# Experts' last tiles cut to 64 tokens, token lists gathered ahead, and the run-time loop moved behind the experts' last product

## The chip, the cores and the metric

The program runs on one core of a Trainium2 chip. The metric is device time in microseconds (us) of one execution; lower is better. The core has a matrix engine (PE, or TensorE), a vector engine (DVE), an activation engine (ACT), a general engine (POOL, which issues the gathers and scatters) and a sync engine (SP, which issues the other transfers), each with its own queue of instructions, and 16 DMA engines.

## The reference

Three layers in a row; what the kernel must compute is this, in float32:

```python
# block attention: 8 batches x 8 heads, 576 positions in chunks of 64, 64 wide
attn = softmax(q_c @ k_c.T / 8);  out = attn @ v_c          # inside a chunk
x = out as [4608 tokens, 512]
# mixture of experts: every token goes to one of 8 experts
logits = x @ w_gate;  expert_idx = argmax(logits);  gate_w = softmax(logits)[expert_idx]
ye = relu(x[mask] @ w1[e]) @ w2[e]                          # 512 -> 1024 -> 512
x = gate_w * ye
# MLP: 512 -> 2048 -> 512, piecewise quadratic activation
h = x @ w_in
g = where(h >= 1, h, where(h <= -1, 0, (h + 1) ** 2 / 4))
out = g @ w_out
```

## The kernel before, in words

Every float32 operand of the expert and MLP products is scaled by a power of two and written as a sum of two fp16 numbers, `high` (L109, on ACT) and `low` (L112, on DVE: the rest after the high part). A product is made of three: high by high, high by low and low by high. Tokens go in tiles of 128.

**Attention** takes 36 steps of 128 tokens. In a step PE makes scores (L456), transposes (`t`, L464; `tx`, L484), the weighted values (`ob`, L476) and the gate's logits (`la`), DVE the maxima and normalised rows (L500 to L520), ACT the exponential `p` (L504). Steps are gathered to seven batches of the gate; after each, DVE works out every token's expert and its place in that expert's list, and POOL scatters the token numbers into the lists (L617).

**Experts** are taken by rank, the sizes being known only at run time. The token tiles are cut into 13 windows (rank r, first tile k, number of tiles): (0,0,3), (0,3,3), (1,0,4), (2,0,3), (2,3,3), (3,0,4), (4,0,3), (4,3,3), (5,0,4), (6,0,3), (6,3,2), (7,0,3), (7,3,2); they are called w0 to w12 here. `CAPS` holds each rank's tiles. `fetch(w)` gathers the list (L163) and the tokens' rows (`xg`, L140), takes the row maxima (`xam`, L100), scales and splits them (`xh`, L109 and L112), and the transposed tiles `xtw` come by DMA (L159). `ffn` then makes a window's first layer, 8 groups of 12 matmuls (L932), each left by ACT (`ht` high, L937) and DVE (`ht` low, L938), and its second layer, 24 matmuls of 512 columns to a tile (L966). `leave` copies a tile out of PSUM (ACT, L954), takes its maximum (`ym`, DVE) and scatters it (POOL, L958); in most windows this is done in the window behind.

Beside the windows a planner runs generators (`background`) that fetch and split the experts' weights, fetch the next window, and load the MLP's weights (`load_mlp`). Instructions are placed in the queues in the order in which the planner lets them go, by modelled clocks of the engines (`clk`), prices (`yield`, `spend`) and constants: `LIST` and `ROWS` are the modelled landing times of a list and of the rows. `load_mlp` ends in 16 conversions: `high` of a row of `mlpw`, then `low`, and then only the next row's `high`, since it writes over the row that the `low` before reads.

Tokens above an expert's cap go through `overflow()`, a loop whose trip count is read at run time (L992, L994). Every engine meets at a barrier there. With the reference's inputs the experts hold, by rank, 649, 506, 688, 452, 657, 417, 621 and 618 tokens, so that the loop makes no trip. Before the loop all of `background` is drained into the queues: `before_last` does so and calls `overflow`. The loop stands between the two layers of w12. The MLP (L1117, L1145) follows, in ten groups.

Of the kernel before, what the change touches and what calls it, by code (L numbers as in the profile page):

```python
# [29 lines left out]
CAPS = (6, 4, 6, 4, 6, 4, 5, 5)  # L30
BATCH = (6, 6, 6, 4, 6, 5, 3)
# [9 lines left out]
LIST, ROWS, WEIGHTS = 2.2, 3.0, 4.5  # L41
SLACK = 0.3, 0.6
# [12 lines left out]
def build(ctx, tc, qT, kT, v1, wg, w1, w2, wi, wo, out):  # L55
# [12 lines left out]
    with tc.manual_schedule(engines={E_.PE, E_.Activation, E_.DVE, E_.SP}):  # L68
# [114 lines left out]

        def fetch(w):

            r, k, size = windows[w]
            if k == 0 or w == 1:
                yield 0.1, 0.0
                spend(0.0, 0.0, 1.05)
# [9 lines left out]
            at = [clk["pool"] + ROWS - 1.05 * (size - 1 - t) for t in range(size)]  # L199
# [154 lines left out]
        with ExitStack() as ph:  # L354
# [70 lines left out]
            for r in range(E):  # L425
                pool.memset(capt[:, r:r + 1], float(CAPS[r] * P))
# [60 lines left out]
            def vector_work(i):  # L487
# [39 lines left out]
                if 0 <= i - 4 < NT:  # L527
# [3 lines left out]
                    spend(0.0, 0.65)  # L531
                slot(1.15)
                yield

            la = ps_l.tile([P, 512], F32, name="la")
            acc = la[:, 128:128 + (GB + 1) * E].rearrange("p (t e) -> p t e", e=E)
# [9 lines left out]
            def by_token(i):  # L546

                b, t = WHERE[i]
                if t == 0:
                    LG[b] = la[:, b % 2 * 64:b % 2 * 64 + GB * E].rearrange("p (t e) -> p t e", e=E)  # L550
                pe.matmul(LG[b][:, t, :], lhsT=LT.pop(i), rhs=sel4, start=True, stop=True)

            def gate(b):
                n = BATCH[b]
                lg = LG.pop(b)[:, 0:n]
# [188 lines left out]
        def gate_tail():  # L744
# [18 lines left out]
            ready[0] = 2  # L763
            for _ in range(20):
                yield
            overflow_plan()
# [3 lines left out]
        def overflow_plan():  # L770
# [5 lines left out]
            dve.tensor_tensor(out=nr, in0=nr, in1=capt, op=ALU.subtract)  # L776
# [3 lines left out]
            dve.tensor_scalar(out=nw, in0=nr, scalar1=float(P - 1), scalar2=0.0, op0=ALU.add, op1=ALU.max)  # L780
# [66 lines left out]
        with ExitStack() as ph:  # L847
# [71 lines left out]
            def ffn(r, xt, nt, ids, gates, i_x, beside=None, after=None, last=False, between=None, c0=0):  # L919

                N = nt * P
# [23 lines left out]
                if between:  # L945
                    between()
# [3 lines left out]
                ys = [ps_y.tile([P, 512], F32, name=f"y{t}", tag=f"y{t}") for t in range(min(nt, 3))] + more_ys[:max(0, nt - 3)]  # L950

                def leave(t):
                    y = yp.tile([P, D], F32, name="y", tag="y")
                    act.activation(out=y, in_=ys[t], func=AF.Copy, scale=gt[:, t:t + 1])  # L954
                    ym = small.tile([P, 1], F32, name="ym", tag="ym")
                    absmax(ym, y)
                    dve.tensor_tensor(out=ymax, in0=ymax, in1=ym, op=ALU.max)
                    ins = pool.indirect_dma_start(out=yd, out_offset=bass.IndirectOffsetOnAxis(ap=ids[t], axis=0), in_=y, in_offset=None,  # L958
# [17 lines left out]
                if not last:  # L976
# [10 lines left out]
            def overflow():  # L987
# [6 lines left out]
                with tc.For_i(0, n_over, 1):  # L994
# [9 lines left out]
                    dve.scalar_tensor_tensor(out=tmp, in0=capt, scalar=1.0 / P, in1=csum[:, 0:E], op0=ALU.mult, op1=ALU.subtract)  # L1004
# [29 lines left out]
                    ffn("over", xt, 1, [ix[:, 0:1]], ix[:, 1:2].bitcast(F32), i_x, last=True, c0=c_over)  # L1034
# [167 lines left out]
```

## Time and profile before

| | |
|---|---|
| three runs | 1375.74, 1376.52 and 1385.33 us; median 1376.52 |
| the profiled execution | 1387.27 us, its span 1385.3 us |
| PE busy | 1325.9 us, 96% of the span |
| DVE, ACT, POOL busy | 55%, 43%, 11% |
| granted PE clock, mean | 0.985 of full speed |
| stages | attention to about 190 us, experts to 634, MLP to the end |

The span is what the trace covers; the execution's own time is 2 us longer. The profiled execution lies 10.75 us above the median of the three runs, and one of the three is as long. The trace shows which engine an idle engine waited for; as PE is busy nearly throughout, its few idle stretches are the first thing to look for, and the rate of its products the second.

### The profile page before, as it was taken

What the parts mean: (1) busy time and instruction counts of PE and PEld (TensorE: products, weight loads), DVE (VectorE), ACT (ScalarE), POOL (GpSimd) and SP (SyncE); (2) the same over time, 40 slices, a digit from 0 to 9 for tenths busy, and PEclk for the clock granted to TensorE, in tenths of its full rate; (3) what the DMA queues carried; (4) which work ended last, traced back from release to release, by engine and by line L of the source; (5) the groups of instructions that cost most, each with busy time, mean ns of one, the idle gap of its engine ahead of it and who ended that gap; (6) DMA issues with size and microseconds to landing.
All of it is one profiled execution on the core that took longest, in us unless ns stands there. A gap on an engine that the chain in (4) does not pass through costs nothing.

```text
span 1385.3 us, 20006 instructions
## 1 busy us (share of the span) xinstructions
PE 1325.9 (96%) x7735; PEld 697.8 (50%) x7735; DVE 766.2 (55%) x1545; ACT 593.9 (43%) x1000; POOL 151.9 (11%) x190
## 2 busy tenths in 40 slices
PE   7888788999999999989999999999999999999998
PEld 5666653445445445555444444444444444444555
DVE  5558655678678777756464270724518064370723
ACT  3446433666666766644242240413315042240522
POOL 3111231221231222310000000000000000000000
PEclk9999899999999999999999999999999999999999
DMA  9989636666667663312111111111110111111000
GB/s 242 286 265 279 161 91 197 206 206 232 192 204 239 174 207 109 98 52 77 31 53 31 62 22 35 35 31 61 31 61 1 31 61 31 54 23 37 22 26 16
DMA packets 123201, 147.99 MB, mean 107 GB/s; under 512 B 89164, under 2 KB 89164, under 8 KB 121056
## 3 DMA queue, kind: packets, MB, share of 16 engines
q1 hardware_dynamic: 115264, 127.40, 32.6%
q0 software_dynamic: 7840, 19.29, 4.1%
q8 instruction: 62, 1.02, 0.3%
q14 instruction: 35, 0.29, 0.1%
HBM read 99.10 MB, written 29.72 MB: 93 GB/s over the span
## 4 chain that ended last, share of the span: by engine, by line
PE 55%; ACT 0%; issue 0%
PE h L1117 27%; PE o L1145 27%; PE y L966 1%; ACT y L954 0%; ACT ot L1138 0%
## 5 line engine op out<-in xcount | busy, mean ns | idle before, releaser
L1117 PE MATMUL h<-xtw,mlpw 128*128 128x512 f16 (+2 forms) x1920 | 375.1, 358 | 0.8 <-ACT y L954 0.8
L1145 PE MATMUL o<-mlpw,gt 128*128 128x512 f16 x1728 | 374.6, 379 | 0.0
L1122 DVE SCALAR_TENSOR_TENSOR q<-r,kf_g 128x512 f32<-128x512 f32 (+2 forms) x160 | 111.7, 698 | 363.7 <-ACT r L1120 363.7
L1117 PEld LDWEIGHTS <-mlpw 128*128 128x128 f16 x1920 | 187.8, 98 | 187.0 <-issue 1.1
L1145 PEld LDWEIGHTS <-gt 128*128 128x128 f16 x1728 | 169.2, 98 | 203.3
L932 PE MATMUL h<-xtw,wt 128*128 128x384 f16 (+2 forms) x1248 | 213.5, 332 | 14.5 <-DMA xtw<-xh 9.9
L966 PE MATMUL y<-wt,ht 128*128 128x512 f16 x960 | 212.2, 383 | 5.6 <-DVEq L994 5.6
L1120 ACT ACTIVATE r<-h,b_g,a_g 128x512 f32<-128x512 f32 (+2 forms) x160 | 117.6, 735 | 184.9 <-PE h L1117 182.4
L932 PEld LDWEIGHTS <-wt 128*128 128x128 f16 x1248 | 122.4, 99 | 103.6 <-DMA xtw<-xh 10.9
L966 PEld LDWEIGHTS <-ht 128*128 128x128 f16 x960 | 94.5, 99 | 120.0 <-issue 9.6
L1138 ACT ACTIVATE ot<-o,io_g 128x512 f32<-128x512 f32 x36 | 24.0, 688 | 289.7 <-PE o L1145 283.6
L1123 DVE SCALAR_TENSOR_TENSOR q<-h,c_g,q 128x512 f32<-128x512 f32 (+2 forms) x160 | 111.7, 698 | 5.7
L1110 DVE TENSOR_TENSOR gt<-q,gt 128x512 f16<-128x512 f32 (+2 forms) x160 | 100.6, 629 | 1.1 <-ACT gt L1109 0.2
L1109 ACT ACTIVATE gt<-q 128x512 f16<-128x512 f32 (+2 forms) x160 | 92.2, 576 | 10.2 <-DVE q L1123 10.2
L112 DVE SCALAR_TENSOR_TENSOR wt<-raw,s_w,wt 128x1024 f16<-128x1024 f32 x64 | 79.4, 1278 | 8.5 <-ACT wt L109 8.5
L109 ACT ACTIVATE wt<-raw,s_w 128x1024 f16<-128x1024 f32 x64 | 70.5, 1139 | 31.6 <-DVE i_w L89 25.5
L938 DVE SCALAR_TENSOR_TENSOR ht<-h,ht 128x384 f16<-128x384 f32 (+2 forms) x104 | 58.3, 562 | 43.7 <-ACT ht L937 42.1
L106 ACT ACTIVATE wt<-raw 128x1024 bf16<-128x1024 f32 x64 | 66.9, 1048 | 5.1 <-DMA raw<-w 5.1
L937 ACT ACTIVATE ht<-h 128x384 f16<-128x384 f32 (+2 forms) x104 | 50.3, 491 | 43.2 <-PE h L932 37.0
L958 POOL DMA_INDIRECT yd<-y,list x40 | 42.2, 1055 | 92.5 <-ACT y L954 84.8
L456 PE MATMUL s<-kbd,qt 128*64 128x128 f32 x576 | 44.9, 303 | 6.6 <-DMA kbd<-kT 6.5
L476 PE MATMUL ob<-vbd,pt 128*64 128x130 f32 x576 | 45.7, 296 | 5.2 <-issue 5.2
(160 smaller groups left out, 907.4 us busy)
## 6 DMA issues: line engine op xcount, KB each, us to landing
raw<-w SPq DMA_DIRECT2D x64, 512.0 KB
vbd<-v SPq DMA_DIRECT2D x36, 260.0 KB
xd<-xr SPq DMA_DIRECT2D x18, 512.0 KB
xg<-yd SPq DMA_DIRECT2D x36, 256.0 KB
out<-ot SPq DMA_DIRECT2D x36, 256.0 KB
qt<-qT SPq DMA_DIRECT2D x16, 512.0 KB
kbd<-kT SPq DMA_DIRECT2D x32, 256.0 KB
mlpw<-w_in SPq DMA_DIRECT2D x8, 1024.0 KB
```

The source lines that it names most:

```text
L106: act.activation(out=junk, in_=src, func=AF.Square, accum_out=ss)
L109: act.activation(out=hi, in_=src, func=AF.Copy, scale=s)
L112: dve.scalar_tensor_tensor(out=lo, in0=src, scalar=s, in1=hi, op0=ALU.mult, op1=ALU.subtract)
L932: pe.matmul(h[:, 0:N], lhsT=wa[:, a, wc:wc + P], rhs=xt[:, 4 * b + dc, 0:N], start=n == 0, stop=n == 11)
L966: pe.matmul(ys[t], lhsT=ht[:, a, f, c0 + t * P:c0 + (t + 1) * P], rhs=wb[:, b, f * D:(f + 1) * D], start=f == 0 and n == 0, stop=f == 7 an ...
L1109: act.activation(out=gt[:, 0, f, 0:N], in_=q, func=AF.Copy)
L1110: dve.tensor_tensor(out=gt[:, 1, f, 0:N], in0=q, in1=gt[:, 0, f, 0:N], op=ALU.subtract)
L1117: pe.matmul(h[:, 0:N], lhsT=w_in(a, dc, f), rhs=yt[:, 4 * b + dc, 0:N], start=n == 0, stop=n == 11)
L1120: act.activation(out=r, in_=h[:, 0:N], func=AF.Relu, scale=ci["a"], bias=ci["b"])
L1122: dve.scalar_tensor_tensor(out=q, in0=r, scalar=ci["sq"], in1=r, op0=ALU.min, op1=ALU.mult)
L1123: dve.scalar_tensor_tensor(out=q, in0=h[:, 0:N], scalar=ci["c2"], in1=q, op0=ALU.mult, op1=ALU.max)
L1145: pe.matmul(os_[t], lhsT=gt[:, a, f, t * P:(t + 1) * P], rhs=w_out(b, f), start=f == 0 and n == 0, stop=f == 15 and n == 2)
```

## The change

Five things change. (1) `TOKENS` takes the place of `CAPS * 128`: ranks 0, 2 and 4 are capped at 704 tokens and rank 5 at 448, so that the last tile of w1, w4, w7 and w8 holds 64 tokens. Their first layer has `N` = 320 columns instead of 384 (448 instead of 512 in w8); the second layer's last tile gives 64 rows, from as many matmuls of 512 columns. (2) `fetch` gathers the next rank's list behind a window's rows, straight from `lidx`; the copy `li` on DVE is gone; for w0 the modelled landing times are `LIST0` and `ROWS0`. (3) ACT copies the gate's logits out of PSUM (`leave_bank`, seven times) and the gate's DVE work reads the copy. (4) `overflow_plan` goes from the start of `fetch(1)` to behind w2. (5) w11's second layer goes by tile and each tile leaves at once; `first_rows` (the MLP's first rows: scale, loads, splits, transposes) is put into the background of w12; the draining of the background and the loop go from between w12's layers to behind its last product.

```diff
+TOKENS = (704, 512, 704, 512, 704, 448, 640, 640)
 LIST, ROWS, WEIGHTS = 2.2, 3.0, 4.5
+LIST0, ROWS0 = 4.0, 9.0
...
+        def get_it(r):
+            spend(0.0, 0.0, 1.05)
+            lists[r] = get_list(lidx[:, r:r + 1])
...
-                li = small.tile([P, 1], I32, name="li", tag="li")
-                dve.tensor_copy(out=li, in_=lidx[:, r:r + 1] if r else lidx0)
-                lists[r] = get_list(li)
+            if w == 0:
+                yield 0.0, 0.0, 1.05
+                lists[r] = get_list(lidx0)
+                yield 0.0, 0.0, 0.0, clk["pool"] + LIST0
...
+            if w and r < E - 1 and (k == 0 or w == 1):
+                get_it(r + 1)
-            at = [clk["pool"] + ROWS - 1.05 * (size - 1 - t) for t in range(size)]
+            at = [clk["pool"] + (ROWS if w else ROWS0) - 1.05 * (size - 1 - t) for t in range(size)]
...
+            def leave_bank():
+                for b, src in list(LG.items()):
+                    if full[b]:
+                        lg = LG[b] = gsm.tile([P, GB, E], F32, name="lg", tag="lg")[:, 0:BATCH[b]]
+                        act.activation(out=lg, in_=src[:, 0:BATCH[b]], func=AF.Copy)
...
             background.insert(0, fetch(1))
             urgent.append(background[0])
-            ready[0] = 2
-            for _ in range(20):
-                yield
-            overflow_plan()
...
-            def ffn(r, xt, nt, ids, gates, i_x, beside=None, after=None, last=False, between=None, c0=0):
-                N = nt * P
+            def ffn(r, xt, nt, ids, gates, i_x, beside=None, after=None, last=False, between=None, c0=0, y0=0, by_tile=False, N=None):
+                N = N or nt * P
...
-                if between:
-                    between()
...
-                for f, t in sorted(order, key=lambda ft: ft[1]) if last else order:
+                for f, t in sorted(order, key=lambda ft: ft[1]) if last or by_tile else order:
                     for n, (a, b) in enumerate(((0, 0), (0, 1), (1, 0))):
-                        pe.matmul(ys[t], lhsT=ht[:, a, f, c0 + t * P:c0 + (t + 1) * P], rhs=wb[:, b, f * D:(f + 1) * D],
+                        pe.matmul(ys[t][0:min(P, N - t * P)], lhsT=ht[:, a, f, c0 + t * P:c0 + min(N, (t + 1) * P)], rhs=wb[:, b, f * D:(f + 1) * D],
                                   start=f == 0 and n == 0, stop=f == 7 and n == 2)
-                    if last:
+                    if by_tile:
                         if f == 7:
+                            leave(t)
+                            spend(0.75, 0.6, 1.05)
+                        if f % 2 and (t, f) < (nt - 1, QUIET):
+                            beside(6 * 0.215)
+                    elif last:
+                        if f == 7:
+                            if between and t == nt - 1:
+                                between()
                             leave(t)
...
             def before_last():
                 while background:
                     advance()
-                while leaving:
-                    leave_one()
                 overflow()
-                now(first_rows())
...
                 def after(n):
                     leave_one()
+                    if final and n == 0:
+                        background.insert(0, first_rows())
...
-                ffn(r, xt, size, ids, gates, inv, beside, after, final, before_last if final else None)
+                ffn(r, xt, size, ids, gates, inv, beside, after, final, before_last if final else None, by_tile=w == len(windows) - 2, N=min(size * P, TOKENS[r] - k * P))
+                if w == 2:
+                    overflow_plan()
```

Where the planner now puts things is seen in the queues. First ACT, from w12's first layer to the loop. Before, where L109 `mlpw` is a conversion's high part, L937 leaves w12's first layer and L992 to L994 are the loop:

```order
L109 ACTIVATE mlpw<-mlpw,s_m_5799 128x1024 [waits DVE_49,Activation_49]
L937 ACTIVATE ht<-h_2428 128x256 [waits PE_49]
L937 ACTIVATE ht<-h_2844 128x256 [waits PE_49]
L937 ACTIVATE ht<-h_2429 128x256 [waits PE_49]
L109 ACTIVATE mlpw<-mlpw,s_m_5799 128x1024 [waits DVE_49,Activation_49]
L937 ACTIVATE ht<-h_2427 128x256 [waits PE_49]
L937 ACTIVATE ht<-h_2428 128x256 [waits PE_49]
L109 ACTIVATE mlpw<-mlpw,s_m_5799 128x1024 [waits DVE_49,Activation_49]
L992 TENSOR_LOAD trips [waits DVE_49]
L994 COMPARE_AND_BRANCH
L994 UNCONDITIONAL_BRANCH [waits Activation_49]
```

And in the changed kernel, where L111 is the high part, L978 the leaving of w12's first tile and L1024 to L1026 the loop (a row with x3 or x8 stands for as many):

```order
L111 ACTIVATE xh<-xg_90,s_y_6419 128x512 [waits DMAHW5_49,DMAHW2_49]
L962 ACTIVATE ht<-h_2446 128x256 [waits PE_49]
L111 ACTIVATE xh<-xg_91,s_y_6419 128x512 [waits DMAHW6_49,DMAHW3_49]
L111 ACTIVATE mlpw<-mlpw,s_m_6355 128x1024 [waits DVE_49,Activation_49]
L962 ACTIVATE ht<-h_2447 128x256 [waits PE_49]
L978 ACTIVATE y<-y_6521,gt_6519 128x512 [waits DMASW0_49,DVE_49,PE_49]
L111 ACTIVATE mlpw<-mlpw,s_m_6355 128x1024 [waits DVE_49,Activation_49]
L111 ACTIVATE mlpw<-mlpw,s_m_6355 128x1024 [waits DVE_49] x3
L111 ACTIVATE mlpw<-mlpw,s_m_6324 128x1024 [waits DVE_49] x8
L1024 TENSOR_LOAD trips [waits DVE_49]
L1026 COMPARE_AND_BRANCH
L1026 UNCONDITIONAL_BRANCH [waits Activation_49]
```

One conversion stood between w12's last `ht` and the loop, and none of its tiles had been left; now twelve stand there, all behind the leaving of w12's first tile. The first of the sixteen stood in w9's second layer, and now stands between the leaving of w11's second and third tile. DVE's queue holds the twelve low parts at the same place, behind that tile's `ym`, the low part of the MLP's third row tile and one more low part.

Second PE, at the loop. Before, where L932 is w12's first layer:

```order
L932 LDWEIGHTS wt
L932 MATMUL h_2428<-xtw,wt 128x256
L992 TENSOR_LOAD trips [waits DVE_49]
L994 COMPARE_AND_BRANCH
L994 UNCONDITIONAL_BRANCH [waits PE_49]
L994 UNCONDITIONAL_BRANCH [waits barrier_Pool_Activation_PE_DVE_SP_release]
```

And in the changed kernel, where L990 is w12's second layer:

```order
L990 LDWEIGHTS ht
L990 MATMUL y_6522<-wt,ht 128x512
L1024 TENSOR_LOAD trips [waits DVE_49]
L1026 COMPARE_AND_BRANCH
L1026 UNCONDITIONAL_BRANCH [waits PE_49]
L1026 UNCONDITIONAL_BRANCH [waits barrier_Pool_Activation_PE_DVE_SP_release]
```

The loop's barrier stood ahead of w12's second layer (48 matmuls) and now stands behind it, ahead of the MLP.

Third DVE in the last steps of attention, where `mx` opens a step and `xam` is the row maximum of a gathered tile of w0. Before, in the 32nd step:

```order
L500 TENSOR_REDUCE mx<-s 128x8 [waits PE_49]
L503 TENSOR_TENSOR p<-s,mx 128x512 [waits DVE_49]
L516 TENSOR_SCALAR rd<-ob 128x8 [waits PE_49]
L518 RECIPROCAL rd<-rd 128x8 [waits DVE_49]
L520 TENSOR_TENSOR xr<-ob,rd 128x512 [waits DVE_49]
L100 TENSOR_REDUCE xam<-xg_89 128x1 [waits DMASW7_49]
L100 TENSOR_REDUCE xam<-xg_90 128x1 [waits DMASW0_49]
```

And in the changed kernel, in the 34th:

```order
L515 TENSOR_REDUCE mx<-s 128x8 [waits PE_49]
L518 TENSOR_TENSOR p<-s,mx 128x512 [waits DVE_49]
L531 TENSOR_SCALAR rd<-ob 128x8 [waits PE_49]
L533 RECIPROCAL rd<-rd 128x8 [waits DVE_49]
L535 TENSOR_TENSOR xr<-ob,rd 128x512 [waits DVE_49]
L102 TENSOR_REDUCE xam<-xg_89 128x1 [waits DMASW7_49]
L619 RECIPROCAL tok<-sm 128x6
```

The first two `xam` stood behind the 32nd step's rows and the third behind the 33rd's; they now stand behind the 34th's and in and behind the 35th.

## Rows read from the trace of the kernel before

**Rows 1.** Waits of PE: waited for, total us, times, longest us.

```profile
PE t L464 <- ACT p L504: 12.3, 6, 6.0
PE h L932 <- DMA xtw<-xh: 9.9, 2, 6.9
...
PE y L966 <- DVEq L994: 5.6, 1, 5.6
...
PE h L932 <- DVE ht L938: 4.1, 3, 1.7
```

**Rows 2.** Chain that ended last: start, us, what.

```profile
634.07 0.70 ACT y L954
...
697.25 41.44 PE h L1117 x192
```

**Rows 3.** PE timeline in attention's tail: start, us, operation, count, [idle before <-releaser].

```profile
149.67 0.66 PE L464 MATMUL t<-ident,p 128*128 128x128 f32 x4
...
153.43 0.66 PE L464 MATMUL t<-ident,p 128*128 128x128 f32 x4
...
154.45 1.11 PE L476 MATMUL ob<-vbd,pt 128*64 128x130 f32 x16
...
163.32 1.12 PE L464 MATMUL t<-ident,p 128*128 128x128 f32 x4 [6.03 <-ACT p L504]
...
172.45 1.11 PE L476 MATMUL ob<-vbd,pt 128*64 128x130 f32 x16
```

**Rows 4.** DVE timeline at the same place.

```profile
158.70 0.69 DVE L100 TENSOR_REDUCE xam<-xg 128x1 f32<-128x512 f32 x1 [5.72 <-DMA xg<-xd,list]
160.60 0.69 DVE L100 TENSOR_REDUCE xam<-xg 128x1 f32<-128x512 f32 x1 [1.21 <-DMA xg<-xd,list]
```

**Rows 5.** Ten us of windows: busy PE, PEld, DVE, ACT, POOL, clock, DMA.

```profile
160.00:170.00 10.00, 6.68 (x61) 5.61 (x63) 8.65 (x28) 4.03 (x9) 0.00 (x0) 0.50 0.06 24
```

**Rows 6.** PE timeline, windows w1, w10, w11, w12 and the MLP's start.

```profile
233.36 17.71 PE L932 MATMUL h<-xtw,wt 128*128 128x384 f16 x96 [6.91 <-DMA xtw<-xh]
...
549.31 10.64 PE L932 MATMUL h<-xtw,wt 128*128 128x256 f16 x96
559.79 10.52 PE L966 MATMUL y<-wt,ht 128*128 128x512 f16 x48
573.30 15.77 PE L932 MATMUL h<-xtw,wt 128*128 128x384 f16 x96 [2.99 <-DMA xtw<-xh]
...
604.45 10.64 PE L932 MATMUL h<-xtw,wt 128*128 128x256 f16 x96
620.65 13.38 PE L966 MATMUL y<-wt,ht 128*128 128x512 f16 x48 [5.56 <-DVEq L994]
634.81 31.36 PE L1117 MATMUL h<-xtw,mlpw 128*128 128x384 f16 x192 [0.78 <-ACT y L954]
```

**Rows 7.** DVE timeline while PE waits for w1's tiles.

```profile
219.11 0.69 DVE L100 TENSOR_REDUCE xam<-xg 128x1 f32<-128x512 f32 x1 [6.12 <-DMA xg<-xd,list]
...
219.84 0.16 DVE L772 SCALAR_TENSOR_TENSOR base<-ei,base 128x8 f32<-128x8 f32 x1
...
222.71 0.14 DVE L785 CAST trips<-csum 1x1 int32<-1x1 f32 x1
...
229.49 0.74 DVE L112 SCALAR_TENSOR_TENSOR xh<-xg,s_x,xh 128x512 f16<-128x512 f32 x1
```

**Rows 8.** ACT timeline: conversions of the MLP's weights.

```profile
598.42 1.15 ACT L109 ACTIVATE mlpw<-mlpw,s_m 128x1024 f16<-128x1024 f32 x1 [1.35 <-DVE mlpw L112]
600.92 1.15 ACT L109 ACTIVATE mlpw<-mlpw,s_m 128x1024 f16<-128x1024 f32 x1 [1.35 <-DVE mlpw L112]
...
614.51 1.15 ACT L109 ACTIVATE mlpw<-mlpw,s_m 128x1024 f16<-128x1024 f32 x1 [1.53 <-DVE mlpw L112]
...
617.67 1.15 ACT L109 ACTIVATE mlpw<-mlpw,s_m 128x1024 f16<-128x1024 f32 x1 [1.47 <-DVE mlpw L112]
```

**Rows 9.** DVE timeline: the last low part before the loop.

```profile
618.85 1.28 DVE L112 SCALAR_TENSOR_TENSOR mlpw<-mlpw,s_m 128x1024 f16<-128x1024 f32 x1 [0.94 <-ACTq L994]
```

More of the change, by code (lines that the diff above doesn't have):

```diff
@@ L425, in build @@
             for r in range(E):
-                pool.memset(capt[:, r:r + 1], float(CAPS[r] * P))
+                pool.memset(capt[:, r:r + 1], float(TOKENS[r]))
+            capf = const.tile([P, E], F32, name="capf")
+            for r in range(E):
+                pool.memset(capf[:, r:r + 1], float(TOKENS[r] // P))
             base = const.tile([P, E], F32, name="base")
@@ L531, in vector_work @@
                     spend(0.0, 0.65)
+                leave_bank()
                 slot(1.15)
@@ L535, in build @@
             la = ps_l.tile([P, 512], F32, name="la")
+            full = {}
             acc = la[:, 128:128 + (GB + 1) * E].rearrange("p (t e) -> p t e", e=E)
@@ L551, in by_token @@
                 pe.matmul(LG[b][:, t, :], lhsT=LT.pop(i), rhs=sel4, start=True, stop=True)
+                full[b] = t == BATCH[b] - 1
+            def leave_bank():
[3 more added lines that the diff above has]
+                        act.activation(out=lg, in_=src[:, 0:BATCH[b]], func=AF.Copy)
+                        full[b] = False
+                        spend(0.0, 0.25)
             def gate(b):
                 n = BATCH[b]
-                lg = LG.pop(b)[:, 0:n]
+                lg = LG.pop(b)
                 m = gsm.tile([P, GB, 1], F32, name="m", tag="m")[:, 0:n]
@@ L775, in overflow_plan @@
             dve.tensor_reduce(out=nr, in_=g, axis=AX.X, op=ALU.add)
-            dve.tensor_tensor(out=nr, in0=nr, in1=capt, op=ALU.subtract)
+            more = const.tile([P, E], F32, name="more")
+            dve.tensor_tensor(out=more, in0=nr, in1=capt, op=ALU.is_gt)
+            dve.scalar_tensor_tensor(out=nr, in0=capf, scalar=-float(P), in1=nr, op0=ALU.mult, op1=ALU.add)
             csum = const.tile([P, E + 1], F32, name="csum")
@@ L779, in overflow_plan @@
             nw = const.tile([P, E], I32, name="nw")
-            dve.tensor_scalar(out=nw, in0=nr, scalar1=float(P - 1), scalar2=0.0, op0=ALU.add, op1=ALU.max)
+            dve.scalar_tensor_tensor(out=nw, in0=nr, scalar=float(P - 1), in1=more, op0=ALU.add, op1=ALU.mult)
             dve.tensor_scalar(out=nw, in0=nw, scalar1=7, scalar2=None, op0=ALU.logical_shift_right)
@@ L975, in ffn @@
                             beside(3 * 0.215)
-                if not last:
+                if not last and not by_tile:
                     leaving.extend((leave, t) for t in range(nt))
@@ L1033, in overflow @@
                     now(columns([xg], xt, [s_x]))
-                    ffn("over", xt, 1, [ix[:, 0:1]], ix[:, 1:2].bitcast(F32), i_x, last=True, c0=c_over)
+                    ffn("over", xt, 1, [ix[:, 0:1]], ix[:, 1:2].bitcast(F32), i_x, last=True, c0=c_over, y0=2)
                     dve.tensor_scalar(out=jt, in0=jt, scalar1=1.0, scalar2=None, op0=ALU.add)
@@ L1065, in after @@
                     leave_one()
+                    if final and n == 0:
+                        assert not leaving
+                        background.insert(0, first_rows())
                     if more and n == 8:
```

24 lines of the change are left out of this document (14 added, 10 removed).

## The prediction

> **What bounds the kernel now.** I read the waits of PE first, because PE is the engine whose end sets the end: the chain that ended last is PE's products, one half-group of the MLP behind the other, 41.44 us each, back to the leaving of w12's last tile at 634.07 [rows 2]. Nothing of the MLP is changed, so only what comes ahead of its first product can move the time, and there only three things: stretches in which PE stands, products that run at the slow clock, and products that are left out. The waits give the first [rows 1]: ACT's `p` in attention (one of 6.0), the transposed tiles `xtw` (6.9 and 3.0), the loop (5.6), and the lows of `ht` (three, 4.1 together). The PE timeline gives each its place and shows the second: after the long stops the same products take longer [rows 3, 6], and the row of the windows that holds the first of them shows a granted clock of 0.50, which is the 1.2 GHz level [rows 5].
>
> **Part A, attention's tail.** PE stands 6.03 us before the transposes at 163.32, for ACT's `p` [rows 3]. ACT is not the cause: `p` needs a subtraction that DVE makes, and DVE stood 5.72 us on the first `xam` of w0 and 1.21 on the second, until the gathered rows had landed at 158.70 and 160.60 [rows 4]. The change puts the first `xam` two steps further back. A step takes 3.76 us at full rate (149.67 to 153.43) [rows 3], so DVE would come there at about 160.5 (two steps behind 152.97, the end of its last work before the wait: 158.70 less 5.72), 1.8 us after the rows have landed. The stop should go, and with it the slow clock behind it: from 163.32 to 172.45 is 9.13 us, against 4.78 for the same operations from 149.67 to 154.45 [rows 3]. That is 6.03 + 4.35 = 10.4 us. What is late next: w0's `xh` and transposes, which come two steps (7.5 us) later against the steps around them. The trace shows no wait of PE for w0's tiles, so I put nothing on it; if they came last, 2.9 of the 10.4 would be left. Bounds: nothing to 10.4.
>
> How much of it is in the median run is the hard question. The profiled execution took 1387.27 us, the median run 1376.52; one run of the three took 1385.33. The step between these, about 10 us, is the size of this stop with its slow clock, and a wait for a gather among other transfers is the kind of thing that differs from run to run. But the trace holds one execution, and nothing in it says that the short runs lack the stop. I keep both ends and take the middle.
>
> **Part B, window 1.** PE stands 6.91 us for w1's last transposed tile, and its first layer then takes 17.71 us instead of the 15.77 of w11 [rows 6]: at most 8.9 us. DVE's work on the way: the first `xam` at 219.11, then the overflow plan from 219.84 to 222.85 while the other tiles land, then the other two `xam`, and the last low at 229.49, with lows of the weights between [rows 7]. The change takes the plan out (3.0 us) and puts the three lows in a row. I take 3.0; the upper bound is 8.9, the lower zero (if the last tile's landing and not DVE is what comes last). The plan now stands behind w2, where PE waits for nothing that it holds up. The first part of the stop, the list's gather behind SP's seven raw loads, stays: those loads stand at the same place of SP's queue.
>
> **Part C, narrower products.** 96 products of 384 columns take 15.77 us and 96 of 256 take 10.64 [rows 6]: 5.13 us for 128 columns, 2.57 for 64. Four windows lose 64 columns: 10.3 us. The second layer still streams 512 columns in as many products, so nothing there. The bounds are nothing and 10.3; I take the whole, since the rate between the two widths is the rate that I need.
>
> A product of 512 columns takes 10.52 / 48 = 219 ns here [rows 6]. The Trainium skill, "TensorE: Matmul & The Clock Gate", section "Back-to-back issue gap", has it otherwise: in a stream of weight load and product pairs the spacing is about 81 ns at 128 columns and 131 ns at 512, an estimate of 8.3 ns for 64 columns. By that the 384 products would give back 3.2 us instead of 10.3 and the sum below would come out at 1384; the trace does not agree with it.
>
> **Part D, waits for `ht`.** Three waits, 4.1 us [rows 1]. A narrower product leaves ACT and DVE less work to a group, but PE too, and the copy `li` that stood among them goes. Two of the three, 2.5 us, lie in windows that change; between 0 and 2.5 I take 1.3.
>
> **Part E, w11's tiles.** PE stands 2.99 us at 573.30 for w11's transposes [rows 6]. The list is now gathered one window ahead, which in w10 takes the copy, the list's landing and the wait for it off the way to the rows. I take 2.99, bounds 0 and 2.99. On POOL the list's gather stands ahead of some scatters, about 1.0 us each; nobody waits for those in the windows.
>
> **Part F, the loop.** Before, the loop cost 5.56 us of standing between w12's layers, and the products behind it 13.38 us instead of 10.52 [rows 6]. Now it comes after the last product, and the queue of ACT holds twelve conversions ahead of it, all behind the leaving of w12's first tile; DVE holds their lows. This is the term that decides. Conversions follow one another strictly, high, low, next high: two in a row stand 2.50 us apart [rows 8], 1.15 of ACT, 1.28 of DVE and the hand-overs. I count from F, the start of w12's first layer. Before, the MLP's first product comes at 634.81 - 604.45 = F + 30.4. After: the second layer starts at F + 10.5 (559.79 - 549.31), and its first tile, now made first, is ready half of 10.52 later, F + 15.7 [rows 6]. It is left in 0.70 [rows 2], its maximum takes 0.69, as an `xam` of the same shape does, a row tile's low 0.74 [rows 7], the conversion's low that is still owed 1.28 [rows 9]: F + 19.2. Twelve pairs at 2.50 make F + 49.2. From the last low to PE's going on it was 0.5 before (618.85 + 1.28, then 620.65) [rows 6, 9], the leaving of the second tile, which stands behind the barrier, takes 0.70, and the MLP starts after a long stop, so I put the 2.86 us (13.38 - 10.52) of the slow clock on it: F + 53.2. The loss is 22.9 us. PE stands idle from F + 21 to F + 50, some 29 us. Without the slow clock it would be 20.0. What hid these conversions before is PE's products of w11 and w12; that cover is gone, because `load_mlp` has fallen so far behind that they begin only while w11's tiles leave.
>
> `leave_bank` adds seven copies of 48 elements on ACT in attention. PE's work hides them, so I put nothing on them; without that cover each costs no more than the 0.70 us of a copy of 512 [rows 2], 4.9 us in all.
>
> **The sum.** Gains 10.4 + 3.0 + 10.3 + 1.3 + 3.0 = 28.0, loss 22.9: 5.1 us less. From the profiled 1387.3 this gives 1382.2; from the median 1376.5, where it holds stop A too, 1371.4, and where it doesn't, 1376.5 - 17.6 + 22.9 = 1381.8. I take the middle of the last two, 1377. A measurement of this kernel can tell about 1% from no change, 13.8 us here (1362.8 to 1390.3), so this forecast is no change.
>
> **The rivals.** First, faster: the stop at w1 goes whole with its slow clock (8.9 instead of 3.0), the `ht` waits too (1.2 more), the MLP starts at full clock (2.9), and A is in the median: 1371.4 - 10.0 = 1361.4. For it speaks that a stop cut to half may no longer lower the clock; against it that four things must all come right. Chance 0.17.
>
> Second, slower: the drained conversions do not go at 2.50. Among other work of ACT and DVE the last two before the loop began 3.16 us apart, at 614.51 and 617.67 [rows 8]; twelve at that pace cost 7.9 more, 1389.7 where A is not in the median. From 3.2 us on it is over the bound, and at 3.5 it is 1394. Against it: behind the leaving of the first tile no other work stands between them in either queue, as between 598.42 and 600.92. The first part of the chain can be late as well, since the MLP's row loads now stand in w12's first layer, ahead of DVE's lows of `ht`. Chance 0.14.
>
> Third, the change does not do what it says: an expert over its cap would send the loop round, with eight loads of weights and their eight conversions, 20 us at the pace above, 1397 or more. The experts' counts are below every cap, so 0.01. That rule on narrow products would give 1384 and takes 0.03.
>
> **How the numbers follow.** The forecast takes the 0.65 that is left, its own time between 1371 and 1382. Range: the faster rival's 1361.4 and the unknown part of C pull the ends out; I leave out about 1 in 10 on each side, 1360 to 1389. Faster by over 1% 0.17, within 1% 0.68 (forecast and the rule's case), slower 0.15.
>
> **What the changed profile would show.** Right: no stop on `p` in attention's tail and a clock near full there; w1's stop about 4 us; 96 products of 320 columns in 13.2 us; no stop at w11; and, new, one stop of about 29 us on the loop behind the last product of w12, with eight or more conversions in a row on ACT, 2.50 us apart. Wrong: conversions done by the time of w12's first layer (then the time is 1348 to 1359), or a pace above 3 us.

## The result, and the profile after

The changed kernel takes 1392.91 us (median of 4 runs, 1392.03 to 1396.76), the kernel before 1378.64 (4 runs, 1375.74 to 1385.33). The ratio is 1.0115, with a 95% interval of 1.0078 to 1.0151: some 14 us slower, where no change was forecast (1377, range 1360 to 1389). The profiled execution took 1393.42 us, its span 1391.7.

The waits of PE in the changed kernel (as in [rows 1]):

```profile
PE h L1151 <- ACT y L978: 29.5, 1, 29.5
PE t L479 <- ACT p L519: 15.0, 9, 5.2
PE h L957 <- DMA xtw<-xh: 11.5, 3, 7.4
PE la L561 <- ACT lg L576: 7.0, 1, 7.0
```

The stop at the loop is there as forecast: 29.5 us. Against [rows 1], `ht` is no longer waited for, but the stops on `p` and `xtw` have not gone, and one on `lg`, the new copy of the gate's logits, has come. PE's timeline gives their places (as [rows 3] and [rows 6]):

```profile
141.85 0.66 PE L479 MATMUL t<-ident,p 128*128 128x128 f32 x4
...
150.87 1.11 PE L479 MATMUL t<-ident,p 128*128 128x128 f32 x4 [5.18 <-ACT p L519]
...
173.16 0.66 PE L479 MATMUL t<-ident,p 128*128 128x128 f32 x4 [0.93 <-ACT p L519]
...
181.76 0.90 PE L957 MATMUL h<-xtw,wt 128*128 128x384 f16 x3 [2.81 <-DMA xtw<-xh]
...
224.29 15.90 PE L957 MATMUL h<-xtw,wt 128*128 128x320 f16 x96 [7.37 <-DMA xtw<-xh]
240.03 17.39 PE L990 MATMUL y<-wt,ht 128*128 128x512 f16 x72
258.72 20.88 PE L957 MATMUL h<-xtw,wt 128*128 128x512 f16 x96 [1.30 <-DMA xtw<-xh]
...
331.29 13.20 PE L957 MATMUL h<-xtw,wt 128*128 128x320 f16 x96
...
588.41 10.64 PE L957 MATMUL h<-xtw,wt 128*128 128x256 f16 x96
598.89 10.52 PE L990 MATMUL y<-wt,ht 128*128 128x512 f16 x48
638.93 33.26 PE L1151 MATMUL h<-xtw,mlpw 128*128 128x384 f16 x192 [29.52 <-ACT y L978]
```

A stop of 5.18 us on `p` stands at 150.87. In [rows 3] the stop stood at 163.32, two steps further on. w0's first product waits 2.81 us for its transposes, w1's 7.37, and w2's 1.30, where w2 did not wait before. 96 products of 320 columns take 13.20 us, as forecast. But w1's second layer takes 17.39 us for the 72 products that took 15.70. From F (588.41) to the MLP's first product it is 50.5 us, and that product's group then takes 33.26 us instead of 31.36 [rows 6].

ACT's timeline shows the conversions in front of the loop, and, ahead of them, the gate's copy:

```profile
82.58 1.06 ACT L108 ACTIVATE wt<-raw 128x1024 bf16<-128x1024 f32 x1 [9.87 <-DMA raw<-w]
...
83.79 0.20 ACT L576 ACTIVATE lg<-la 128x48 f32<-128x48 f32 x1
...
604.27 0.69 ACT L978 ACTIVATE y<-y,gt 128x512 f32<-128x512 f32 x1 [3.90 <-PE y L990]
607.84 1.15 ACT L111 ACTIVATE mlpw<-mlpw,s_m 128x1024 f16<-128x1024 f32 x1 [2.89 <-DVE mlpw L114]
610.34 1.15 ACT L111 ACTIVATE mlpw<-mlpw,s_m 128x1024 f16<-128x1024 f32 x1 [1.35 <-DVE mlpw L114]
...
635.35 1.15 ACT L111 ACTIVATE mlpw<-mlpw,s_m 128x1024 f16<-128x1024 f32 x1 [1.35 <-DVE mlpw L114]
638.20 0.69 ACT L978 ACTIVATE y<-y,gt 128x512 f32<-128x512 f32 x1 [1.71 <-DVEq L1026]
```

w12's first tile is left at 604.27, and behind it the twelve conversions stand 2.50 us apart, 607.84 to 635.35, up to the loop (as [rows 8]). At 82.58 ACT had waited 9.87 us for a raw weight; the copy `lg` stands behind that work, and the gate waits for it.

The profile of before lies 10.75 us above the median of the first three runs. The first experiment gives a profile of the same kernel nearer to it, and with that the places where time was won and lost can be told.

### The profile page after: what moved, and what is told of

It reads as the page before. It is cut to its first block, busy times and chain, and to the rows that moved or that the text cites. A ratio compares the mean times of both kernels' runs of the same rounds, so it can differ in the third digit from the quotient of the medians.

```text
span 1391.7 us, 20008 instructions
## 1 busy us (share of the span) xinstructions
PE 1312.2 (94%) x7735; PEld 687.9 (49%) x7735; DVE 764.5 (55%) x1537; ACT 595.8 (43%) x1007; POOL 152.8 (11%) x198
## 4 chain that ended last, share of the span: by engine, by line
PE 54%; ACT 0%; issue 0%; ACTq 0%
PE h L1151 27%; PE o L1179 27%; ACT y L978 0%; ACT ot L1172 0%; ACTq L1026 0%
## 5 line engine op out<-in xcount | busy, mean ns | idle before, releaser
L1151 PE MATMUL h<-xtw,mlpw 128*128 128x512 f16 (+2 forms) x1920 | 377.0, 359 | 29.5 <-ACT y L978 29.5
L990 PE MATMUL y<-wt,ht 128*128 128x512 f16 (+1 forms) x960 | 216.1, 380 | 0.0
L957 PE MATMUL h<-xtw,wt 128*128 128x384 f16 (+4 forms) x1248 | 203.7, 325 | 11.5 <-DMA xtw<-xh 11.5
L990 PEld LDWEIGHTS <-ht 128*128 128x128 f16 (+1 forms) x960 | 90.2, 99 | 122.3 <-issue 23.4
L1143 ACT ACTIVATE gt<-q 128x512 f16<-128x512 f32 (+2 forms) x160 | 92.2, 576 | 10.2 <-DVE q L1157 10.2
L963 DVE SCALAR_TENSOR_TENSOR ht<-h,ht 128x384 f16<-128x384 f32 (+4 forms) x104 | 56.4, 543 | 52.7 <-ACT ht L962 52.1
L962 ACT ACTIVATE ht<-h 128x384 f16<-128x384 f32 (+4 forms) x104 | 49.7, 478 | 69.4 <-PE h L957 69.1
L111 ACT ACTIVATE wt<-raw,s_w 128x1024 f16<-128x1024 f32 x64 | 70.4, 1140 | 20.0 <-DVE s_w L90 11.7
L142 POOL DMA_INDIRECT xg<-xd,list x40 | 48.2, 1206 | 61.1 <-DVE xh L114 22.1
L644 POOL DMA_INDIRECT ld<-tok,slot x36 | 35.5, 986 | 121.0 <-DVE slot L642 72.7
```

Source lines behind the costliest of these rows:

```text
L111: act.activation(out=hi, in_=src, func=AF.Copy, scale=s)
L957: pe.matmul(h[:, 0:N], lhsT=wa[:, a, wc:wc + P], rhs=xt[:, 4 * b + dc, 0:N], start=n == 0, stop=n == 11)
L990: pe.matmul(ys[t][0:min(P, N - t * P)], lhsT=ht[:, a, f, c0 + t * P:c0 + min(N, (t + 1) * P)], rhs=wb[:, b, f * D:(f + 1) * D], start=f == ...
L1143: act.activation(out=gt[:, 0, f, 0:N], in_=q, func=AF.Copy)
L1151: pe.matmul(h[:, 0:N], lhsT=w_in(a, dc, f), rhs=yt[:, 4 * b + dc, 0:N], start=n == 0, stop=n == 11)
```

## The experiments

### The kernel before again

No edit.

> The kernel before, unchanged, profiled once more. If the stop of 6.03 us on ACT's p in attention's tail belongs to every run, it is there again at the same step and the time is near 1387; if it comes and goes with the landing of the gathered rows, the profile shows it shorter or gone, w0's first product comes up to 10 us before 189.85, and the time is near 1376.

Measured: 1379.67 us over 10 runs (1374.85 to 1385.65); the profiled execution took 1376.3. PE's timeline:

```profile
141.12 0.66 PE L464 MATMUL t<-ident,p 128*128 128x128 f32 x4
...
157.91 1.11 PE L464 MATMUL t<-ident,p 128*128 128x128 f32 x4 [5.45 <-ACT p L504]
...
164.78 1.11 PE L476 MATMUL ob<-vbd,pt 128*64 128x130 f32 x16
...
171.47 0.66 PE L464 MATMUL t<-ident,p 128*128 128x128 f32 x4 [0.21 <-ACT p L504]
...
177.12 0.65 PE L932 MATMUL h<-xtw,wt 128*128 128x384 f16 x3
...
220.76 18.59 PE L932 MATMUL h<-xtw,wt 128*128 128x384 f16 x96 [9.08 <-DMA xtw<-xh]
239.19 15.70 PE L966 MATMUL y<-wt,ht 128*128 128x512 f16 x72
...
560.57 17.45 PE L932 MATMUL h<-xtw,wt 128*128 128x384 f16 x96 [3.11 <-DMA xtw<-xh]
...
593.40 6.82 PE L932 MATMUL h<-xtw,wt 128*128 128x256 f16 x61
...
623.92 31.36 PE L1117 MATMUL h<-xtw,mlpw 128*128 128x384 f16 x192 [0.78 <-ACT y L954]
```

(The last row but one is the start of w12; the view ends behind its 61st product.) The stop on `p` (5.45 us) is there at the 33rd step in this short execution too, so it belongs to both. What makes the execution of the first profile longer is only in small part this stop. w0's first product comes 12.7 us later there (189.85 against 177.12). Of this, 4.8 us are there before the stop, at the 32nd step's transposes (153.43 against 148.64). 2.9 us come in the stop and the slow clock behind it: the operations that took 9.13 us there [rows 3] take 6.87 here (157.91 to 164.78), so that stop and slow clock are 7.5 us here and 10.4 there. And 5.1 us come behind. PE's waits in the first profile have 9.7 us in short stops put down to "issue" (nothing that the profile shows was waited for), and in this one none. The same kind of stop, 8.7 to 12.0 us in all, is in the profiles of the last four experiments and in none of the others. Why it comes is open.

With this profile the whole difference of the spans, 1391.7 - 1374.4 = 17.3 us, is told by places (the differences are those of the unrounded times):

| | before (this run) | changed | difference |
|---|---|---|---|
| start of w0 | 177.1 | 181.8 | +4.6 |
| w0 to w1 | 43.6 | 42.5 | -1.1 |
| w1 to w12 (F) | 372.6 | 364.1 | -8.5 |
| F to the MLP | 30.5 | 50.5 | +20.0 |
| MLP | 750.5 | 752.8 | +2.3 |

### The MLP's weights ahead of the experts'

```diff
-                    background.append(load_mlp())
+                    background.insert(0, load_mlp())
```

> The changed kernel with the MLP's loading put at the front of the planner's background, so that the sixteen conversions stand well ahead of the loop. If the stop of 29.5 us behind the last product is the queue of twelve conversions, it falls to 1 to 3 us and the time to about 1393 - 27 - 2 (slow clock at the MLP's start) = 1364, within 1361 to 1369. If the barrier itself is dear where it now stands, some 5 us of it stay (1369 or more). If ACT and DVE, loaded earlier, hold up the experts' weights, new waits in the windows take part of the gain.

Measured: 1409.80 us, ratio 1.0200 to before (1.0148 to 1.0252). PE at the MLP's start, and its waits:

```profile
660.61 33.05 PE L1151 MATMUL h<-xtw,mlpw 128*128 128x384 f16 x192 [2.14 <-DVE inv_g L834]
```

```profile
PE y L990 <- ACT wt L111: 14.2, 3, 6.1
...
PE y L990 <- DVE wt L114: 10.0, 3, 6.1
...
PE h L957 <- DVE wt L114: 6.0, 2, 3.7
```

The stop of 29.5 us is now 2.14: it was the conversions. But the time of ACT and DVE that it takes is now missing for the experts' weights `wt`, which PE waits for from w2 to w6, 30.2 us in these three rows. The planner's background is full; work put forward pushes other work back.

### The gate's logits from PSUM again

```diff
-                leave_bank()
                 slot(1.15)
...
-                lg = LG.pop(b)
+                lg = LG.pop(b)[:, 0:n]
```

> The changed kernel without ACT's copies of the gate's logits: DVE reads them from PSUM again. If the copy is what made the stop at 84 us, because it stands in ACT's queue behind a square that waits for the first weights, the stop falls from 7.0 to about 3.4 us or less, its slow clock gets shorter, and the time falls by 3 to 6 us to 1387 to 1390. If the stop is the landing of the weights alone, it stays at 7 and the time within 2 us of 1393.

Measured: 1398.03 us, ratio 1.0122 (1.0073 to 1.0171), so not faster. The stop at that place is 4.06 us. Over all profiles it was 2.7 to 4.1 us in the six without the copy and 2.0 to 8.0 in the eight with it (means 3.3 and 5.6). But the traces do not show the copy holding PE up. The stop ends by the landing of the first weights, in all fourteen profiles: from the start of ACT's work on the landed weight to PE's next product it is 1.46 to 1.47 us with the copy (82.58 to 84.04 in the changed kernel) and 2.05 to 2.06 without it (81.54 to 83.59 in `e0_before`). So the copy takes 0.6 us off that way, and the long stop of the changed kernel is an early arrival: PE came there at 77.0, in `e0_before` at 79.9. This run lost its time at w2, where PE waited 3.07 us instead of 1.30 and the products behind ran slower: w3 starts 4.2 us later (304.30 against 300.15), and the spans differ by 4.0.

### 128 stationary columns in the last tiles

```diff
-                        pe.matmul(ys[t][0:min(P, N - t * P)], lhsT=ht[:, a, f, c0 + t * P:c0 + min(N, (t + 1) * P)], rhs=wb[:, b, f * D:(f + 1) * D],
+                        pe.matmul(ys[t], lhsT=ht[:, a, f, c0 + t * P:c0 + (t + 1) * P], rhs=wb[:, b, f * D:(f + 1) * D],
```

> The changed kernel with the second layer's last tile of w1, w4, w7 and w8 made from 128 columns of ht again (the rows above 64 are not used), the first layer as narrow as it is. If 64 stationary columns are what makes 72 products take 17.39 us and not 15.70, they take 15.70 again and the time falls by 4 x 1.7 = 6.7 us to 1386. If something else of these windows does it, they stay at 17.39 and the time stays.

Measured: 1388.88 us over 10 runs, ratio 1.0072 (1.0052 to 1.0093). w1's second layer:

```profile
242.01 15.70 PE L990 MATMUL y<-wt,ht 128*128 128x512 f16 x72
```

It takes 15.70 us again, as do w4's and w7's. So a product from 64 stationary columns costs more, not less: 1.69 us for 24 of them, 70 ns each. The narrow stationary tiles of four windows had given back 6.8 us of the 10.2 that their first layers had won. The time fell by 4.0 us, and all ten runs (1387.00 to 1391.24) lie below the four of the changed kernel. The rest is lost elsewhere in this execution: w0 starts 1.8 us later, w2's stop is 1.2 us longer (2.51), and the MLP's first group takes 1.0 us more (34.28).

### No loop

```diff
-                overflow()
```

> The changed kernel without the run-time loop (tokens above a cap would be left out; there are none), the draining of the conversions as it is. If the stop behind the last product is the conversions, it stays near 29 us and the time near 1392. If it is the barrier of the loop, most of it goes and the time falls by 20 us or more.

Measured: 1398.01 us, one run, in which w2's stop was 5.62 us and not 1.30. PE at the MLP's start:

```profile
643.03 34.35 PE L1150 MATMUL h<-xtw,mlpw 128*128 128x384 f16 x192 [27.70 <-ACT y L978]
```

27.70 us of the stop stay without the loop. By this one run the barrier is worth 1.8 us there, the conversions the rest.

### The copy of w0's index put back

```diff
-                yield 0.0, 0.0, 1.05
-                lists[r] = get_list(lidx0)
+                yield 0.1, 0.0
+                spend(0.0, 0.0, 1.05)
+                li = small.tile([P, 1], I32, name="li", tag="li")
+                dve.tensor_copy(out=li, in_=lidx0)
+                lists[r] = get_list(li)
```

In the changed kernel POOL's queue holds the list's gather ahead of `ag_w`, the maximum by which the weights are scaled; before, `ag_w` came first. POOL's timeline of the changed kernel, and then DVE's, at the new stop:

```profile
145.87 0.98 POOL L165 DMA_INDIRECT list<-ld,lidx  x1 [4.79 <-DMA vbd<-v]
146.89 0.31 POOL L105 PARTITION_ALL_REDUCE ag_w<-am_w  x1
```

```profile
147.23 0.15 DVE L79 TENSOR_SCALAR kb<-ag_w 128x1 int32<-128x1 int32 x1 [5.83 <-POOL ag_w L105]
```

The gather waits 4.79 us for transfers, `ag_w` runs behind it at 146.89, and DVE has waited 5.83 us for that, with the next steps' work behind it in its queue.

> The changed kernel with the copy of the first list's index on DVE put back for w0 alone, which puts POOL's maximum of the weights ahead of the list's gather again, as before the change; the later row maxima of w0 stay. If that gather is what made the stop of 5.2 us in attention's tail, the stop goes with its slow clock, w0's first product comes 5 to 9 us sooner (173 to 177) and the time falls to 1384 to 1388. If the stop is the landing of transfers whatever stands in POOL's queue, it stays and the time is 1393 within 2.

Measured: 1388.56 us over 5 runs, ratio 1.0078 (1.0045 to 1.0111). PE's timeline:

```profile
146.43 0.66 PE L482 MATMUL t<-ident,p 128*128 128x128 f32 x4
...
170.71 0.66 PE L482 MATMUL t<-ident,p 128*128 128x128 f32 x4 [0.93 <-ACT p L522]
...
179.24 1.12 PE L960 MATMUL h<-xtw,wt 128*128 128x384 f16 x3 [2.74 <-DMA xtw<-xh]
```

No long stop on `p` is left in attention's tail (behind the 30th step the longest is 0.93 us): from the 30th step's transposes to the 36th's it is 24.3 us (146.43 to 170.71), against 31.3 (141.85 to 173.16) in the changed kernel with the stop at the 31st. The 30th step came 4.6 us later in this execution, so that w0 started only 2.5 us sooner. w0 still waits 2.74 us for its transposes. The interval of the ratio overlaps that of the changed kernel, so what the stop is worth is read from these places and not from the time.

### The planner's slack

`SLACK` is how far, in modelled us, another engine's clock may run ahead of PE's before the planner holds work back; its second number holds behind attention.

```diff
-SLACK = 0.3, 0.6
+SLACK = 0.3, 0.8
```

> The changed kernel with one of the planner's numbers, the slack behind attention, at 0.8 and not 0.6: four conversions and not twelve stand behind the leaving of w12's first tile, and none of the experts' weights is put late. If each conversion there costs 2.50 us, the stop falls by 8 x 2.5 = 20 us to about 9.5 and the time to 1373, within 1370 to 1377. If the stop is of the loop, it stays and so does the time.

Measured: 1380.15 us over 10 runs, ratio 1.0022 (1.0005 to 1.0039): 13 us less than the changed kernel, where 20 were expected. PE's timeline:

```profile
263.72 16.59 PE L957 MATMUL h<-xtw,wt 128*128 128x512 f16 x69 [5.83 <-DMA xtw<-xh]
...
624.80 33.25 PE L1151 MATMUL h<-xtw,mlpw 128*128 128x384 f16 x192 [6.95 <-ACT y L978]
```

The stop at the loop fell by 22.6 us, to 6.95, where eight conversions fewer were expected to take off 20; four stand behind the leaving of w12's first tile. From F to the MLP it is 29.9 us instead of 50.5. Where the rest went is w2: its stop was 5.83 us in this execution, and the products behind it ran at a lower granted clock (0.70 from 256 to 266), so that w3 started 6.5 us later than in the changed kernel.

### All of it

128 stationary columns, the copy of w0's index and slack 0.8 as above, `load_mlp`'s pieces asked for 2.0 us ahead instead of 5.0, and the background drained ahead of w12's second layer:

```diff
+                if between:
+                    drain()
                 wb, u = ranked[r]() if callable(ranked[r]) else ranked[r]
```

> The changed kernel with what the runs point to: the copy for w0's list put back, 128 stationary columns in the second layer's last tiles, slack 0.8, the MLP's pieces asked for sooner, and the background drained ahead of w12's second layer, so that three conversions run beside its products. If the reasons are right, the stop at the loop falls to 1 to 4 us and the gains of the other parts are there: from e6's 1373 less 7 for the loop, 5 for the stationary columns, 4 to 8 for w0's list: 1352 to 1360, below both kernels. If new waits take their place, it is above 1365.

Measured: 1367.73 us over 6 runs, ratio 0.9917 (0.9887 to 0.9946): below both kernels, but not by as much as expected. PE at the MLP's start, and POOL:

```profile
615.20 34.05 PE L1158 MATMUL h<-xtw,mlpw 128*128 128x384 f16 x192 [8.07 <-ACT y L983]
```

```profile
609.91 1.01 POOL L987 DMA_INDIRECT yd<-y,list  x1 [19.36 <-ACTq L1035]
615.57 0.99 POOL L987 DMA_INDIRECT yd<-y,list  x1 [4.65 <-ACT y L983]
```

DVE's last low of a conversion ends at 608.72, PE's last product ends at 607.13, and DVE's work on w12's first tile at 610.54, but the loop's barrier lets ACT go on only at 614.46. What was still under way was the scatter of that tile, which POOL had issued at 609.91: in this run such scatters land 2.2 to 5.1 us after their issue, and 614.46 is 4.55 after. The reading is that POOL meets at the barrier only when its scatter has landed; a new wait had taken the place of the old. No run tests this alone.

### The weights released earlier

```diff
-            if w == 1:
-                yield 0.0, 0.0, 0.0, at[-1]
-                ready[0] = 2
...
             urgent.append(background[0])
+            ready[0] = 2
```

> The changed kernel with the next expert's weights released (ready[0] = 2) where they were before the change, at the start of w1's fetch, so that SP's queue holds three of its raw loads right behind w1's transposes and w2's four transposes in a row again. If the new stop ahead of w2 (1.3 to 5.8 us in the runs so far, with a slow clock behind the longer ones) comes from raw loads among w2's transposes, it goes and the time falls by 2 to 7 us to 1386 to 1391. If it is DVE's order, it stays, and the time is 1393 within 2.

Measured: 1404.93 us, ratio 1.0097 (1.0061 to 1.0132). (For this and the next three experiments the kernel before was measured again and took 1390.86 us, 13 us more than for the others; their ratios are to that. The record has the same chip number for them as for the first four experiments.) PE's timeline:

```profile
238.20 16.15 PE L955 MATMUL h<-xtw,wt 128*128 128x320 f16 x96 [11.15 <-DMA xtw<-xh]
...
271.51 20.89 PE L955 MATMUL h<-xtw,wt 128*128 128x512 f16 x96
```

w2's stop is gone, as expected if it comes from raw loads among w2's transposes. SP's queue bears it out, with w1's three transposes and w2's four:

```profile
227.38 3.10 SPq L161 DMA_TRANSPOSE xtw<-xh  x2
230.68 0.46 SPq L223 DMA_DIRECT2D raw<-w  x1
231.24 1.24 SPq L161 DMA_TRANSPOSE xtw<-xh  x1
...
255.48 6.69 SPq L161 DMA_TRANSPOSE xtw<-xh  x4
```

In the changed kernel w1's three stood in a row (216.69), and a raw load (249.18) stood ahead of w2's fourth. Here w2's four are in a row, but one raw load stands between w1's own, and w1 now waits 11.15 us instead of 7.37. The stop moved by one window, and the ratio cannot be told from that of the changed kernel. So the new stop at w2 came of a part of the change that the five points ahead do not list: this release of the weights had been moved from the start of `fetch(1)` to where w1's rows have landed by the model. In the three runs with the early release w2 has no such stop; in the changed kernel and in `e2_no_bank` to `e7_all` it is 1.30 to 5.83 us.

### The best of the parts

The edits of `e7_all`, `e8_ready` and `e2_no_bank`, and w12's tiles left behind the loop:

```diff
                     elif last:
                         if f == 7:
-                            if between and t == nt - 1:
-                                between()
-                            leave(t)
+                            if t == nt - 1:
+                                if between:
+                                    between()
+                                for u in range(nt):
+                                    leave(u)
```

> The kernel of e7_all, with the weights released as in e8_ready, the gate's logits read from PSUM as in e2_no_bank, and both of w12's tiles left behind the loop, so that no scatter is on its way when the loop's barrier asks for it; all sixteen conversions now stand ahead of w12's last ht. If the 8.07 us stop left in e7_all is the scatter of w12's first tile, it falls to 2 us or less; with w2's stop (5.7) and 2.4 at the gate gone the time falls from 1367.7 to 1353 to 1358. If the barrier itself takes 4 us or more, it is 1358 to 1363.

Measured: 1367.09 us over 6 runs, ratio 0.9833 (0.9801 to 0.9866), 23.8 us less than the kernel before beside it. The expected times went by the kernel before at 1377.9 us, and 0.9833 of that would be 1355, an estimate that takes the ratio to hold there. PE at the MLP's start:

```profile
613.25 33.05 PE L1157 MATMUL h<-xtw,mlpw 128*128 128x384 f16 x192 [2.14 <-DVE ymax L983]
```

2.14 us are left, for DVE's last maximum; ACT goes on at 611.45, 0.34 us behind the end of PE's last product. That no scatter is on its way agrees with the reading of `e7_all`, but the conversions also end sooner here, so the two are not told apart by this run alone.

### w0's rows sooner

```diff
-LIST0, ROWS0 = 4.0, 9.0
+LIST0, ROWS0 = 4.0, 5.0
```

> The kernel of e9_best with ROWS0 at 5.0 and not 9.0, which puts the first row maximum of w0 behind the 33rd step and its splits in the 35th and 36th. If w0's transposes are what PE now waits for (2.6 to 3.0 us in every run of the changed kernel), the time is up to 3 us below e9_best. If the gathered rows land later than the 33rd step, a stop in attention's tail comes back and it is 3 us or more above it.

Measured: 1365.28 us, ratio 0.9821 (0.9785 to 0.9856). The intervals of this and the last overlap widely: no difference that could be measured. There was little to win: w0's transposes, for which PE waited 2.60 to 3.00 us in the runs up to `e7_all`, cost it only 0.47 us in `e9_best` already. Here PE does not wait for them.

### Narrower first layers alone

The kernel before with `TOKENS` and `N` in `ffn`, the second layer as in `e3_wide_last`:

```diff
-                N = nt * P
+                N = N or nt * P
...
-                ffn(r, xt, size, ids, gates, inv, beside, after, final, before_last if final else None)
+                ffn(r, xt, size, ids, gates, inv, beside, after, final, before_last if final else None, N=min(size * P, TOKENS[r] - k * P))
```

> The kernel before with the narrower first layers alone (caps of 704 and 448, last tiles of 64 rows left, the second layer from 128 stationary columns), all else as it was. Its first layers lose 10.3 us. But in its queues twelve conversions stand behind w12's first layer, as in the changed kernel, and one in the kernel before. If the narrower windows alone make the planner late, PE stands about 30 us ahead of w12's second layer where it stood 5.6, and the time is 1378 + 24 - 10 = 1392. If that order costs nothing, it is 1368.

Measured: 1411.43 us, ratio 1.0153 (1.0110 to 1.0197), 20.6 us slower. PE's timeline at the loop, which here still stands between w12's layers:

```profile
641.15 13.05 PE L973 MATMUL y<-wt,ht 128*128 128x512 f16 x48 [30.31 <-DVEq L1001]
```

30.31 us instead of 5.56. The narrower windows alone, without the loop's new place, put the conversions behind. By the kernel's text the planner's model gets less of PE's time from them to put ACT's and DVE's work beside (`beside(3 * N * 0.00042)` at each quarter of a group), and what didn't fit was the last in line, `load_mlp`. The time is above the 14 us more that were expected: in this execution w11's transposes hold PE for 7.76 us, where it was 2.99 and 3.11 in the two profiles of before.

## Why the prediction was wrong

**Part F, the loop, was right.** Forecast: a loss of 22.9 us, PE idle for 29. Measured: 20.0 from F to the MLP and 2.3 in the MLP behind the stop, 22.3 in all, idle 29.5. The pace of 2.50, read from two rows of the kernel before, held for all twelve. The stop is the conversions and not the barrier (the kernel without the loop keeps 27.7). The runs add what the prediction hadn't asked, why the conversions were late: not for the loop's new place but for the narrower windows (they alone, with the loop where it was, bring 30.3).

**Part A failed, and most of the error is there.** The step that failed is "The stop should go": it looked at DVE's queue alone. Its `xam` no longer held DVE, but the list's gather, without the copy that had held it back, moved ahead of `ag_w` on POOL, and DVE stood for that instead, 5.18 us of PE's time where 5.45 had gone. What was put at nothing came as well: w0's transposes came last, 2.81 us. (That this is for the row maxima two steps further back is argued from the order; the one run that moved them forward had only 0.47 us of this wait to lose.) So w0 started 4.6 us later where 0 to 10.4 sooner had been the range. With the copy back (`e5_li0`) the stop is gone, as forecast, and from the 30th step's transposes to w0 it is 32.8 us where the short run of before took 36.0 (141.12 to 177.12): 3.2 gained, near the 2.9 that the prediction gave for the case that w0's transposes come last. The question put beside it, whether the median run holds the stop, was answered by the middle of yes and no: the size of the difference, 10.75 us, fitted the stop with its slow clock (10.4) by chance. The short run holds 7.5 of those 10.4 us as well.

**Part C was mis-sized.** The first layers won 4 x 2.56 = 10.2 us, as forecast (10.3). "The second layer still streams 512 columns in as many products, so nothing there" was the false step: 6.8 us were lost there, so that 3.5 were left (`e3_wide_last`). That is near the 3.2 that the rule of the Trainium skill ("TensorE: Matmul & The Clock Gate", "Back-to-back issue gap") gave, but not for its reason: products of 320 columns stand 13.20 / 96 = 137.5 ns apart, 0.43 ns to a column, as with this trace's 219 ns at 512.

**Part B** was forecast at 3.0, and little of it came: PE went from w0 to w1 in 1.1 us less, and w1's stop is 7.37 us where about 4 was the sign. The plan is gone from DVE, but w1's transposes now land 5.4 us behind the last low (218.93, then 224.29) where it was 3.1 (230.23, then 233.36), and w2 got a stop of its own. In `e8_ready` w2's stop went and w1's grew when the raw loads were moved. Why w1's transposes landed later in the changed kernel is open.

**Parts D and E** held in their numbers: no wait for `ht` is left, nor the stop at w11 (3.11 us in the short run of before, with 1.7 of slow clock behind it, so 4.8 won where 3.0 were forecast). For D this is luck. The prediction put two of the three waits, 2.5 us, in windows that change; they stand in w3 (316.64) and w6 (422.25), whose widths stay, and the third in w0. The short run of before has one, 1.6 us, in w6. What took it away was not tested.

The copies of `leave_bank`, put at nothing, cost nothing that the traces show.

By the short run's numbers: +4.6 instead of about -5 at w0, 3.5 instead of 10.3 from the narrow tiles, the rest close; that is the way from the forecast to what was measured. The slower rival was right in its sign only: its mechanism, a slower pace of conversions, did not happen.

## What to carry to other kernels

A wait that is taken away also held something back: before a wait on one queue is counted as gain, look at what its instruction now overtakes on the next queue, and who waits for that. When work is cut on the engine that bounds, the work that a planner hides beside it can lose room; see what stands last in line and where it will be drained. A tile half as wide must be priced in each product that it enters, with its stationary side as well as its moving side.

## What the hardware showed

A product of 512 columns from 64 stationary columns took 70 ns longer than one from 128 (17.39 against 15.70 us for 72 products of which 24 are such, and 22.56 against 20.88 for 96 in w8). The weight loads of the second layer, by their width, in the changed kernel:

```profile
L990 PEld LDWEIGHTS <-ht 128*128 128x128 f16 x864 | 82.2, 98 | 105.4 <-issue 9.9 <-ACT wt L111 0.8 <-ACT nu L920 0.4
...
L990 PEld LDWEIGHTS <-ht 128*64 128x64 f16 x96 | 7.9, 108 | 17.0 <-issue 13.6
```

A load of 64 columns took 108 ns, one of 128 took 98, so half the columns did not load faster here. Why the product takes 70 ns more was not tried.
